# Halved storage of an intermediate, a planner estimate and filler matmuls in a one-core Fourier and mixture kernel

## The chip, the core and the metric

The kernel runs on one core of a Trainium2 chip. The metric is device time in microseconds (us) of one execution; the kernel before has a median of 672.75 us over 3 runs (670.91 to 673.87). Its engines are TensorE (PE, with its weight loads PEld), VectorE (DVE), ScalarE (ACT), GpSimd (POOL) and SyncE (SP), which issues nearly all DMAs.

## The reference

For each of 8 batches, x (3136 x 256) goes through a Fourier transform along its rows, a complex product with a 256 x 256 weight, a soft threshold, and the inverse transform. Then the 128 rows with the best score pass a small feed-forward network.

```python
X = np.fft.rfft(x, axis=1)
Yr = Xr @ w_r - Xi @ w_i + b_r
Yi = Xr @ w_i + Xi @ w_r + b_i
Yr = np.sign(Yr) * np.maximum(np.abs(Yr) - lam, 0.0)   # Yi likewise
y = np.fft.irfft(Y, n=3136, axis=1)
scores = np.einsum('bsd,d->bs', y, w_gate)
for b in range(8):
    top_idx = np.argpartition(-scores[b], 128)[:128]
    h = np.maximum(xe @ w1, 0.0)
    out[b, top_idx] = y[b, top_idx] + g[:, None] * (h @ w2)
```

## The kernel before, in words

The length 3136 is split as 98 x 32 (n1 and n2). Per batch b the work has these stages, and each has a function:

- `x_side` (line 810) loads x in 8 pieces i of 98 partitions x 4 KB (xt tiles, for b = 0 also the cin tiles); `xsum_side` (827) forms sum u and difference v of the two halves (xu, xv; on DVE for b = 0, on POOL after that).
- `s1` (the function that calls `quarters`, 839) does the 98-point transform of piece i in eight fp32 matmul instructions with the constant `first`; ACT copies the result to an at, ot or ct tile and SP stores it to As in DRAM.
- `a_side` (871) reloads As transposed, one av tile per group g of 6, once all 8 pieces are stored. `s2` (886) does the 32-point transform in 64 small fp32 matmuls (px<-fwd,av); ACT and DVE split the result in two fp32r halves (Xh, Xl).
- `spectral` (938) multiplies by w: eight steps k, each of three fp32r matmuls (py<-wh,Xh and so on); at k % 4 == 3 the threshold follows, with the bias tile, on DVE, ACT and POOL.
- `s2i` (985) is the inverse 32-point transform (s<-Y,bwd); ACT copies four banks to a ct tile (128 partitions x 4 x 256), DVE forms the score's part (junk, Csc), and `put` (1009) stores the tile to Cs in DRAM, 512 KB. `s2it` (1015) does the same for a small rest, Ct (64 KB).
- `c_side` (1045) reloads C in four parts i per batch into one of two cin tiles: two transfers of 48 partitions (16 to 63 and 64 to 111), 384 KB each, and a small one from Ct to partitions 15 and 112. `csum_side` (1058) forms sum and difference (cu, cv) of the halves; `s1i` (1073) does the inverse 98-point transform and stores the result.
- `score` (1030), `select`, `fetch` and `ffn` choose the rows, gather them, run the network and scatter the result.

The order of the instructions on every engine is written by a planner while the kernel is built. Every engine wrapper (`Engine.given`, line 223), `mm` (258) and `ld` (292) adds an estimate to a clock for its engine; a side job (`pump`, 377) is taken when its estimated time has come, and the loop at the end picks the stage with the least cost for PE. In `ld` a transfer costs SP 0.4 us, the wire takes bytes / 300e3 us, and the data land 1.2 us after that; a tile's estimated time is the latest of all that wrote it. All engines then run in that order, with semaphores for the data.

`warm` (1312) puts matmuls on constants into a PSUM tile that nobody reads, as many as fit into an estimated wait of PE:

```python
n = int((t - WARM[1] + (0.0 if spec["t"] >= T else WS2 if w else WS) - t0) / (0.23 if w else 0.44))
if t - t0 < WARM[0] or n < 1:
    return
for name, bufs in (("s", SB), ("py", 2)):
    if open_at(name, bufs) <= t0 + 0.3:
```

Here t0 is the estimated end of PE's last matmul and t that at which the next stage can begin. With `WARM[0]` = 99 it always returns at once. It is called (1409) before the first spectral step and, once all 48 groups are through `spectral`, in the rest.

At the start (1341) the rows 0 to 14 of every xt and cin tile are cleared, the first on DVE, the others on POOL, through the wrappers `vec` and `gps`, so that the estimated time of the tile counts them.

Of the kernel before, what the change touches and what calls it, by code (L numbers as in the profile page):

```python
# [10 lines left out]
F32 = mybir.dt.float32  # L11
# [8 lines left out]
B, S, D = 8, 3136, 256  # L20
N1, N2 = 98, 32
H1 = N1 // 2
P0 = 15
PT = P0 + N1
NJ = 24
# [31 lines left out]
def _tables():  # L57
    w = _dft_rows()
    n2 = np.arange(N2)

    f1 = np.zeros((2, H1, 64))
    for i in range(NP):
        for c in range(2):
            f1[0, :, P0 + 2 * i + c] = w[:H1, EVEN[i], c]
            f1[1, :, 1 + 2 * i + c] = w[:H1, ODD[i], c]
    f1[0, :, P0 + 48] = w[:H1, 0, 0]
    f1[1, :, 0] = w[:H1, 49, 0]

    crow = {}
    for j in range(NJ):  # L70
        for kap in range(2):
            g, p, jj = j // 4, j % 4 // 2, j % 2
            k, i = _freq(j, kap)
            crow[k] = _crow(g, kap, p, jj)
            assert j < 12 or crow[N1 // 2 - k] == crow[k]

    i1 = np.zeros((2, H1, 64))
    for par in range(2):
        o = P0 if par == 0 else 0
        for k in EVEN:  # L80
            for c in range(2):
                i1[par, 2 * crow[k] + c, o:o + H1] = w[par::2, k, c]
        i1[par, 48, o:o + H1] = w[par::2, 0, 0]
    first = np.zeros((128, 2, 2, 64))
    for z, t in enumerate((f1, i1)):
        first[P0:64, z] = (np.roll(t, 1, 1) if z else t).transpose(1, 0, 2)
        first[64:PT, z] = t.transpose(1, 0, 2)

    g = np.zeros((NJ, 2, 2, N2, 2, N2))
    gi = np.zeros((6, 2, 2, 2, N2, 2, 2, N2))  # L90
    for j in range(NJ):
        for kap in range(2):
            kk, _ = _freq(j, kap)
            z = -1.0 if kk % 2 else 1.0
            for s in range(N2):
                k = kk + N1 * s
                sg = 1.0 if 2 * k <= S else -1.0
                a = 2 * np.pi * ((n2 * k) % S) / S
                co, si = np.cos(a), np.sin(a)
                g[j, kap, 0, :, 0, s] = co  # L100
                g[j, kap, 1, :, 0, s] = si
                g[j, kap, 0, :, 1, s] = -sg * si
                g[j, kap, 1, :, 1, s] = sg * co
                v = gi[j // 4, j % 4 // 2, kap, j % 2, s]
                v[0, 0] = 2 * co / S
                v[1, 0] = -2 * sg * si / S
                v[0, 1] = z * 2 * si / S
                v[1, 1] = z * 2 * sg * co / S
    g = g.reshape(NJ, 128, 64).transpose(1, 0, 2)

    gi = gi.reshape(6, 2, 128, 2, 2, N2).transpose(2, 0, 1, 3, 4, 5).reshape(128, NJ, 64)

    fr = [(0, N1 * s) for s in range(1, 16)] + [(1, 49 + N1 * s) for s in range(16)] + [(0, 0), (0, S // 2)]
    gt = np.zeros((2, N2, 97))
    git = np.zeros((64, 2, N2))
    for m, (r, k) in enumerate(fr):
        a = 2 * np.pi * ((n2 * k) % S) / S
        co, si = np.cos(a), np.sin(a)
        edge = m > 30
        gt[r, :, 33 + m] = co  # L120
        git[m, r] = (1.0 if edge else 2.0) * co / S
        if not edge:
            gt[r, :, m] = si
            gt[r, :, 66 + m] = -si
            git[33 + m, r] = -2 * si / S

    wq = np.zeros((25, 4, N1))
    order = np.concatenate([np.arange(0, N1, 2), np.arange(1, N1, 2)])
    for j in range(NJ):
        for kap in range(2):  # L130
            k, _ = _freq(j, kap)
            z = -1.0 if k % 2 else 1.0
            col = 4 * (j // 4) + 2 * kap + j % 2
            for c in range(2):
                wq[col, 2 * (j % 4 // 2) + c] = w[order, k, c] * (z if c else 1.0)
    wq[24, 0] = w[order, 0, 0]
    wq[24, 1] = w[order, 49, 0]
    second = np.concatenate([g.reshape(128, -1), gi.reshape(128, -1)], 1)
    tail = np.zeros((64, 97 + 64))
    tail[:, :97] = gt.reshape(64, 97)  # L140
    tail[:, 97:] = git.reshape(64, 64)
    return [a.astype(np.float32) for a in (first.reshape(128, 256), second, tail, wq)]
# [19 lines left out]
def fourier_moe(ctx: ExitStack, tc: tile.TileContext, x, w_r, w_i, b_r, b_i, wg, w1, w2,  # L162
                t_first, t_second, t_tail, t_wq, t_m, t_dig, outs, cap):
    nc = tc.nc
# [5 lines left out]
    dram = ctx.enter_context(tc.tile_pool(name="scratch", bufs=3, space=bass.MemoryType.DRAM))  # L170
# [245 lines left out]
    bias = c_tile([128, 2, D], F32, "bias")  # L416
    bias_t = c_tile([64, D], F32, "bias_t")
    m2l = c_tile([128, 1], F32, "m2l")
    wq = c_tile([25, 4, N1], F32, "wq")
# [564 lines left out]

    def s2i(b, g):
        if g == 0:
            Cs[b] = dram.tile([6, 4, 128, D], F32, name="Cs"), dram.tile([64, D], F32, name="Ct")
            Csc[b] = new(pool, [128, 25], F32, "Csc")
            vec.memset(Csc[b][:, 24:], 0.0)
        for p in range(2):  # L990
            drain(shrinks.pop((b, g, p)))
        y = Y.pop((b, g))
        banks = [new(ps, [128, D], F32, "s", SB) for _ in range(4)]
        for c in range(2):
            for p in range(2):
                for k in range(4):
                    rows = slice(32 * k, 32 * k + 32)
                    mm(banks[k][64 * p:64 * p + 64], bwd[g][rows, 2 * p + c, :], y[rows, p, c, :], c == 0, c == 1, (32 * k, 64 * p))
        t = new(pool, [128, 4, D], F32, "ct", 3)

        def part(k):
            yield "DVE", [banks[k]]
            score_part(b, banks[k], 4 * g + k)

        for k in range(4):
            evict(t[:, k], banks[k])
            hold(banks[k], "s", side(part(k)))

        def put():
            yield "SP", [t]  # L1010
            ld(Cs[b][0][g].rearrange("k p d -> p k d"), t)
            stored["C", b] = stored.get(("C", b), 0) + 1
        hold(t, "ct", side(put()))

    def s2it(b):
        drain(shrinks.pop((b, "t")))
        y = YT.pop(b)
        p = m_tile([64, D])
        mm(p, tail[:, 97:], y)
        t = new(pool, [64, D], F32, "ctt", 1)  # L1020
        act.copy(out=t, in_=p)
        score_part(b, p, 24, 64)

        def put():
            yield "SP", [t]
            ld(Cs[b][1], t)
            stored["C", b] = stored.get(("C", b), 0) + 1
        hold(t, "ctt", side(put()))

    def score(b):  # L1030
        p = m_tile([25, 128])
        turned(p, Csc[b], ident)
        t = new(pool, [25, 4, N2], F32, "sct")
        vec.tensor_copy(t.rearrange("p q n -> p (q n)"), p)
        yield [t]
        p = m_tile([N1, 2, 16])
        for q in range(4):
            mm(p.rearrange("p a n -> p (a n)"), wq[:, q, :], t[:, q, :], q == 0, q == 3)
        vec.tensor_copy(scores[:, b, :].rearrange("p (i a c) -> p a i c", a=2, c=2),
                        p.rearrange("p a (i c) -> p a i c", c=2))  # L1040

# [3 lines left out]
    def c_side():  # L1045
        for b in range(B):
            for i in range(4):
                n = 4 * b + i
                yield "SP", lambda: max(avail(Cs[b]) - EARLY, read.get(key(cts[n % CB]), 0.0)) \
                    if stored.get(("C", b)) == 7 and unused[0] >= 2 * (n - CB + 1) and (0, 7) in summed else None  # L1050
                t = cts[n % CB]
                c = Cs[b][0].rearrange("(q g) k (p a n) d -> a (g k p) q n d", q=2, a=2, n=16)
                for a in range(2):
                    ld(t[16 + 48 * a:64 + 48 * a], c[a, :, :, 4 * i:4 * i + 4, :])
                ld(t[P0::97], Cs[b][1].rearrange("(q a n) d -> a q n d", q=2, a=2)[:, :, 4 * i:4 * i + 4, :])
                stored["c"] = n

    def csum_side():
# [50 lines left out]
    CS, CM = ((0, 8, 9, 10, 11, 12), (11, 12, 13, 14, 14, 14)),42  # L1109
    FB = .25, .5, .75, 1.25, 1.5, 2, 2.5, 3  # L1110
    CN, K0 = 4,4
    WS, WS2 = 1.5, -0.5
    CY = 5, 8, 8, 8, 8, 8, 8, 8
    CX = 10, 10, 10, 10, 11, 11, 11, 12
    WARM = (99, 0.5)
    SP = False
    TB, T1 = -1.5,0.1
    TE, LV, UR, FS, ES, LA, HP = 0,2,0.5,False,True,3,False
# [131 lines left out]
    def middle():  # L1250
# [4 lines left out]
        if k == 8:  # L1255
# [4 lines left out]
                spectral_t(b)  # L1260
                spec["t"], spec["k"] = t + 1, 0
            return t + 1, max(avail(XT[b]), open_at("py")), run, "f"
        if not {"w", "bias"} <= made or (b, g) not in X or (k == 3 and len(Y) > 1):
            return None

        def run():
# [73 lines left out]

    with tc.manual_schedule():
        for z, t in enumerate(xts + cts):
            (gps if z else vec).memset(t[:P0].rearrange("p a c -> p (a c)") if len(t.shape) == 3 else t[:P0].rearrange("p a c d -> p (a c d)"), 0.0)
        ld(first.rearrange("p z c s -> p (z c s)"), t_first)
        side(x_side())
        side(xsum_side())
# [13 lines left out]
        while True:  # L1360
# [40 lines left out]
            if c[1] > now + 0.4:  # L1401
# [3 lines left out]
                if later and min(later) > now + ahead:  # L1405
                    free["PE"] = min(later) - ahead + 0.01
                    continue
            if spec["t"] >= T or at == 0 and (0, 7) in summed:
                warm(c[1])
            if isinstance(c[2], Thread):  # L1410
                if c[2].rank < 0:
# [42 lines left out]
```

## Time and profile before

| | us |
|---|---|
| median of 3 runs | 672.75 (670.91 to 673.87) |
| the profiled execution, its own time | 677.4 |
| its span, first to last instruction | 675.6 |
| PE busy | 633.5 (94% of the span) |
| PEld, DVE, ACT, POOL busy | 407.6, 387.2, 362.6, 394.7 |
| mean granted TensorE clock | 0.978 |

All rows are of one profiled execution. "Busy" is the time in which an engine has an instruction in work; for PE the ends are modelled, so short pauses can hide in it. [...] A bracket behind an instruction says how long its engine stood idle before it and which event ended that; where the engine named had long been done, it was another, often a DMA.

### The profile page before, as it was taken

To read this page: it belongs to the slowest core of one execution; us is meant where nothing else is said; L and a number is where in the kernel's file an instruction comes from. 1 tells how busy PE (TensorE), PEld (TensorE's weight loads), DVE (VectorE), ACT (ScalarE), POOL (GpSimd) and SP (SyncE) were. 2 spreads that over 40 slices of the span, in tenths; PEclk is the share of its full clock that TensorE was granted. 3 is DMA by queue.
4 is the path that set the end of the run, shared out by engine and by line. 5 is a ranking of instruction groups with operands and counts; after the bars stand their busy time and mean duration, and the time that the engine had idled before them with its cause. 6 is when DMAs were issued, how large, how long until landed. Compare 5 with 4: busy or idle time off the path is not lost.

```text
span 675.6 us, 19258 instructions
## 1 busy us (share of the span) xinstructions
PE 633.5 (94%) x7586; PEld 407.6 (60%) x7586; DVE 387.2 (57%) x1208; ACT 362.6 (54%) x779; POOL 394.7 (58%) x337
## 2 busy tenths in 40 slices
PE   6199999999999999999999999999999998799897
PEld 2055755656665656656556666575666665466696
DVE  6123545444457667664667666654667776465742
ACT  4235555557466555656556565566655655444321
POOL 3068443748487656766667466766644656639421
PEclk9679999999999999999999999999999999899999
DMA  8999787989799998897899998897889778478410
GB/s 271 294 247 302 201 273 225 205 282 332 242 268 279 279 313 250 272 296 252 240 276 273 304 266 278 248 306 190 256 241 248 196 223 224 147 177 232 153 39 17
DMA packets 87700, 162.53 MB, mean 241 GB/s; under 512 B 6877, under 2 KB 62010, under 8 KB 87610
## 3 DMA queue, kind: packets, MB, share of 16 engines
q1 hardware_dynamic: 86554, 159.13, 80.1%
q0 software_dynamic: 1056, 2.17, 1.1%
q8 instruction: 60, 0.98, 0.6%
q14 instruction: 30, 0.25, 0.1%
HBM read 83.23 MB, written 78.12 MB: 239 GB/s over the span
## 4 chain that ended last, share of the span: by engine, by line
PE 79%; DMA 7%; issue 5%; DVE 4%; POOL 2%; ACT 1%; SPq 1%; POOLq 0%; DVEq 0%
PE py L272 44%; PE s L272 25%; PE px L272 9%; DMA xe<-in_moe_w 2%; DMA xt<-in_x 2%; DMA av<-As 2%; DMA cin<-Ct 1%; DMA r<-in_w_r 1%; DVE px L220 1%; SPq L301 1%; POOL out L783 1%; DVE c L220 1%; POOL cv L220 1%; DVE py L220 0%; DVE junk L220 0%
## 5 line engine op out<-in xcount | busy, mean ns | idle before, releaser
L220 POOL TENSOR_TENSOR xu<-xt 113x512 f32<-113x512 f32 x56 | 71.9, 1283 | 170.9 <-PE s L272 135.8
L272 PE MATMUL py<-wh,Xh 128*128 128x512 f32 x384 | 169.8, 442 | 1.7 <-ACT Xh L220 1.2
L272 PE MATMUL py<-wl,Xh 128*128 128x512 f32 x384 | 153.0, 398 | 0.0
L272 PE MATMUL py<-wh,Xl 128*128 128x512 f32 x384 | 152.8, 398 | 0.0
L272 PEld LDWEIGHTS py<-wh,Xh 128*128 128x128 f32 x384 | 72.6, 189 | 82.6 <-issue 61.1
L220 DVE TENSOR_TENSOR Xl<-px,Xh 128x512 fp32r<-128x512 f32 x96 | 61.8, 686 | 80.6 <-ACT Xh L220 80.6
L220 POOL TENSOR_TENSOR cu<-cin 113x512 f32<-113x512 f32 x64 | 82.0, 1282 | 41.5 <-PE s L272 39.0
L220 DVE CUSTOM_DVE_ANT_0 junk<-s,wgb 128x256 f32<-128x256 f32 x192 | 80.7, 420 | 32.3 <-ACT ct L220 16.5
L220 ACT COPY ot<-s 113x512 f32<-113x512 f32 x142 | 76.6, 597 | 40.2 <-PE s L272 33.8
L220 ACT COPY at<-s 113x512 f32<-113x512 f32 x110 | 59.2, 592 | 62.4 <-PE s L272 62.4
L272 PEld LDWEIGHTS py<-wl,Xh 128*128 128x128 f32 x384 | 72.8, 189 | 17.3
L220 POOL TENSOR_TENSOR cv<-cin 113x512 f32<-113x512 f32 x64 | 82.1, 1283 | 0.0
L272 PEld LDWEIGHTS py<-wh,Xl 128*128 128x128 f32 x384 | 73.3, 191 | 10.5 <-DVE Xl L220 0.5
L272 PE MATMUL s<-cu,first 64*64 64x512 f32 (+1 forms) x256 | 74.3, 618 | 5.1 <-DVE Csc L220 3.1
L272 PE MATMUL s<-xu,first 64*64 64x512 f32 (+1 forms) x256 | 73.0, 633 | 5.7 <-DVE xu L220 5.7
L272 PEld LDWEIGHTS px<-fwd,av 64*64 64x64 f32 x3072 | 52.1, 137 | 38.0 <-DMA fwd<-t_second 15.7
L220 ACT COPY ct<-s 128x256 f32<-128x256 f32 (+1 forms) x196 | 59.8, 394 | 23.7 <-PE s L272 21.4
L272 PE MATMUL px<-fwd,av 64*64 64x64 f32 x3072 | 56.9, 223 | 16.7 <-DMA av<-As 15.8
L220 POOL TENSOR_TENSOR xv<-xt 113x512 f32<-113x512 f32 x56 | 71.8, 1283 | 0.0
L272 PE MATMUL s<-cv,first 64*64 64x512 f32 (+1 forms) x256 | 71.2, 618 | 0.3 <-POOL cv L220 0.2
L272 PE MATMUL s<-xv,first 64*64 64x512 f32 (+1 forms) x256 | 71.4, 633 | 0.0
L220 ACT ACTIVATE r<-py,m2l 128x512 f32<-128x512 f32 (+1 forms) x58 | 38.3, 660 | 57.2 <-DVE py L220 57.2
(150 smaller groups left out, 968.1 us busy)
## 6 DMA issues: line engine op xcount, KB each, us to landing
out<-ot SPq DMA_DIRECT2D x64, 392.0 KB
av<-As SPq DMA_DIRECT2D x48, 512.0 KB
Cs<-ct SPq DMA_DIRECT2D x48, 512.0 KB
cin<-Cs SPq DMA_DIRECT2D x64, 384.0 KB
xt<-in_x SPq DMA_DIRECT2D x60, 392.0 KB
As<-at SPq DMA_DIRECT2D x55, 392.0 KB
As<-ot SPq DMA_DIRECT2D x7, 392.0 KB
xe<-in_moe_w SPq DMA_DIRECT2D x16, 128.0 KB
```

Of the source, the lines that this page charges most:

```text
L220: return f(*args, **kw)
L272: return nc.tensor.matmul(out, a, b, start=start, stop=stop)
L301: return (eng or nc.sync).dma_start(out=out, in_=src)
L783: nc.gpsimd.indirect_dma_start(out=outs[b], out_offset=bass.IndirectOffsetOnAxis(ap=idx, axis=0), in_=ye, in_offset=None)
```

## The change

C (Cs and Ct) is stored by halves of n2. The columns of the inverse 32-point tables (`gi`, `git`) are put in another order, so that the partitions of a ct tile go (…, n, half); each store becomes two, one of the even and one of the odd partitions (64 partitions x 4 x 1 KB = 256 KB; Ct 32 KB), and a reload fills partitions 16 to 111 of one half of the cin tile with each of its two transfers of 96 partitions, 384 KB as before. The score reads its columns with a step of two. The clearing of rows is issued past the planner's wrappers, so that it counts in no estimate. `warm` is switched on (0.5 in place of 99, with other offsets) and held back as long as pieces of x are summed and not transformed. The spectral steps no longer wait in the plan for the bias, only those with k % 4 == 3 do.

```diff
+    gi = gi.reshape(128, NJ, 2, 2, 16).swapaxes(3, 4).reshape(128, NJ, 64)
+    git = git.reshape(64, 2, 2, 16).swapaxes(2, 3).reshape(64, 2, N2)
...
-            Cs[b] = dram.tile([6, 4, 128, D], F32, name="Cs"), dram.tile([64, D], F32, name="Ct")
+            Cs[b] = dram.tile([2, 2, 3, 4, 64, D], F32, name="Cs"), dram.tile([2, 32, D], F32, name="Ct")
...
-            ld(Cs[b][0][g].rearrange("k p d -> p k d"), t)
+            for a in range(2):
+                ld(Cs[b][0][g // 3, a, g % 3].rearrange("k p d -> p k d"), t[a::2])
...
-            ld(Cs[b][1], t)
+            for a in range(2):
+                ld(Cs[b][1][a], t[a::2])
...
-            mm(p.rearrange("p a n -> p (a n)"), wq[:, q, :], t[:, q, :], q == 0, q == 3)
+            mm(p, wq[:, q, :], t[:, q, :].rearrange("p (n a) -> p a n", a=2), q == 0, q == 3)
...
-                c = Cs[b][0].rearrange("(q g) k (p a n) d -> a (g k p) q n d", q=2, a=2, n=16)
-                for a in range(2):
-                    ld(t[16 + 48 * a:64 + 48 * a], c[a, :, :, 4 * i:4 * i + 4, :])
-                ld(t[P0::97], Cs[b][1].rearrange("(q a n) d -> a q n d", q=2, a=2)[:, :, 4 * i:4 * i + 4, :])
+                c = Cs[b][0].rearrange("q a g k (p n) d -> q (a g k p) n d", n=16)
+                for q in range(2):
+                    ld(t[16:112, q], c[q, :, 4 * i:4 * i + 4, :])
+                ld(t[P0::97], Cs[b][1].rearrange("a (q n) d -> a q n d", q=2)[:, :, 4 * i:4 * i + 4, :])
...
-    WS, WS2 = 1.5, -0.5
+    WS, WS2 = 0.5,0.3
...
-    WARM = (99, 0.5)
+    WARM = (0.5, 0.3)
...
-        if not {"w", "bias"} <= made or (b, g) not in X or (k == 3 and len(Y) > 1):
+        if "w" not in made or (b, g) not in X or k % 4 == 3 and "bias" not in made or (k == 3 and len(Y) > 1):
...
-            (gps if z else vec).memset(t[:P0]...
+            (nc.gpsimd if z else nc.vector).memset(t[:P0]...
...
-            if spec["t"] >= T or at == 0 and (0, 7) in summed:
+            if spec["t"] >= T or at == 0 and (0, 7) in summed and not xuv:
                 warm(c[1])
```

## Rows read from the trace of the kernel before

**Rows 1.** The page: busy shares, then clock and DMA in 40 slices of the span.
```profile
PE 633.5 (94%) x7586; PEld 407.6 (60%) x7586; DVE 387.2 (57%) x1208; ACT 362.6 (54%) x779; POOL 394.7 (58%) x337
...
PEclk9679999999999999999999999999999999899999
DMA  8999787989799998897899998897889778478410
```

**Rows 2.** Stretches: us, then PE, PEld, DVE, ACT, POOL, clock, DMA share, GB/s.
```profile
200.00:300.00 100.00, 99.54 (x1270) 61.01 (x1263) 65.85 (x235) 61.08 (x134) 70.08 (x57) 1.00 0.94 280
...
600.00:615.00 15.00, 13.41 (x105) 11.40 (x102) 9.12 (x29) 5.40 (x9) 7.67 (x7) 1.00 0.89 187
```

**Rows 3.** Timeline of the first wait: start, duration, engine, line, instruction, idle before.
```profile
16.94 1.05 PE L272 MATMUL s<-xv,first 49*64 49x512 f32 x2
...
23.79 0.93 SPq L301 DMA_DIRECT2D av<-As  x2
...
32.84 1.98 PE L272 MATMUL px<-fwd,av 64*64 64x64 f32 x64 [14.83 <-DMA av<-As]
...
35.97 0.79 PE L272 MATMUL py<-wh,Xh 128*128 128x512 f32 x1 [1.15 <-ACT Xh L220]
```

**Rows 4.** Stretches of one us where the granted clock changes.
```profile
21.00:22.00 1.00, 0.00 (x0) 0.00 (x0) 0.00 (x0) 0.00 (x0) 0.00 (x0) 0.94 0.95 371
...
42.00:43.00 1.00, 1.00 (x64) 1.00 (x64) 0.60 (x1) 0.36 (x1) 0.00 (x0) 0.82 0.93 225
```

**Rows 5.** Timeline of the last reloads of C, on SP, POOL and PE.
```profile
594.03 0.40 SPq L301 DMA_DIRECT2D Cs<-ct  x1
...
597.99 1.29 SPq L301 DMA_DIRECT2D cin<-Cs  x2
...
607.16 1.26 POOL L220 TENSOR_TENSOR cu<-cin 113x512 f32<-113x512 f32 x1 [8.11 <-PE s L272]
...
608.47 1.07 PE L272 MATMUL s<-cu,first 64*64 64x512 f32 x2 [1.44 <-POOL cu L220]
609.69 0.64 PE L272 MATMUL s<-cv,first 64*64 64x512 f32 x1
...
627.19 1.28 POOL L220 TENSOR_TENSOR cu<-cin 113x512 f32<-113x512 f32 x1 [2.02 <-DMA cin<-Ct]
...
628.52 1.07 PE L272 MATMUL s<-cu,first 64*64 64x512 f32 x2 [0.58 <-POOL cu L220]
629.74 0.64 PE L272 MATMUL s<-cv,first 64*64 64x512 f32 x1 [0.15 <-POOL cv L220]
```

**Rows 6.** PE's wait at 583 us and the stretch behind it.
```profile
585.00:600.00 15.00, 13.59 (x103) 6.62 (x103) 6.61 (x26) 8.66 (x20) 8.73 (x8) 0.77 0.58 179
...
586.25 1.08 PE L272 MATMUL s<-cu,first 64*64 64x512 f32 x1 [3.06 <-DVE Csc L220]
```

**Rows 7.** Stretches in which x, As and C are loaded, for their DMA rate.
```profile
5.70:11.00 5.30, 5.30 (x25) 1.97 (x26) 4.01 (x7) 2.09 (x4) 1.25 (x1) 1.00 0.91 292
...
28.00:29.00 1.00, 0.00 (x0) 0.00 (x0) 0.00 (x0) 0.00 (x0) 0.00 (x0) 0.50 1.03 349
...
602.00:605.00 3.00, 3.00 (x28) 3.00 (x27) 2.40 (x8) 1.21 (x3) 0.00 (x0) 1.00 0.98 154
```

**Rows 8.** The chain that ended last: start, duration, engine, tile, instructions.
```profile
36.80 5.06 PE py L272 x11
...
58.44 1.09 PE px L272 x64
...
446.42 1.88 PE s L272 x16
...
451.99 4.40 PE py L272 x18
```

**Rows 9.** SP's issues of C's stores: count, ns at least, median and most.
```profile
L301 SPq DMA_DIRECT2D Cs<-ct x48: 359/382/1332, 67.2 to 594.0; - x48
```

**Rows 10.** The page's groups: weight loads of the py steps, busy us and mean ns.
```profile
L272 PEld LDWEIGHTS py<-wh,Xh 128*128 128x128 f32 x384 | 72.6, 189 | 82.6 <-issue 61.1
```

More of the change, by code (lines that the diff above doesn't have):

```diff
@@ L1342, in fourier_moe @@
         for z, t in enumerate(xts + cts):
-            (gps if z else vec).memset(t[:P0].rearrange("p a c -> p (a c)") if len(t.shape) == 3 else t[:P0].rearrange("p a c d -> p (a c d)"), 0.0)
+            (nc.gpsimd if z else nc.vector).memset(t[:P0].rearrange("p a c -> p (a c)") if len(t.shape) == 3 else t[:P0].rearrange("p a c d -> p (a c d)"), 0.0)
         ld(first.rearrange("p z c s -> p (z c s)"), t_first)
```

## The prediction, made before the changed kernel was run

> **What bounds the kernel now.** I read the page first, then stretches, then the chain and the timelines. PE is busy for 94% of the span, and the DMA engines for eight to nine tenths of most slices [rows 1]. Between 200 and 300 us PE works 99.54 of 100 us, at full clock [rows 2]: there every other engine and every transfer has slack, and only fewer PE instructions or a higher clock could save time. So I look for places where PE waits or runs at half clock. There are three.
>
> The first is the start. PE ends the last transform of the first batch at 16.94 + 1.05 = 18.0 us and stands until 32.84, 14.8 us, because the reload of As, issued at 23.79, lands only then [rows 3]. The granted clock falls at about 21.9 us, 3.9 us into that wait, and is full again only at about 42.4 (0.82 in that us; half before) [rows 4]. In between s2 and the first spectral steps run at half clock.
>
> The second is the tail's use of C. The reload of the last batch is issued at 597.99; POOL forms its first sum only at 607.16 (the PE work its bracket names had long ended, so it waited for the DMA), and PE waits for both halves of it. At 628.52 the same happens again, where POOL names the small load behind the reload of C [rows 5].
>
> The third is a 3.06 us wait for the score's DVE parts at 586.25, which drags the mean clock of 585 to 600 down to 0.77 [rows 6].
>
> **Why C is slow.** From 602 to 605 us, when C is loaded into 48 partitions at a time, the DMA engines are 0.98 busy and move 154 GB/s; As into 128 partitions went at 349 (1.03 busy) and x into 98 at 292 [rows 7]. Busy engines with half the bytes say that the destination holds them up. [...]
>
> **The change, part by part.**
>
> *Reload in transfers of 96 partitions.* Bytes and runs (4 KB) stay. A part of C is 2 x 384 + 16 = 784 KB: 5.1 us at 154 GB/s. The new rate is not in the trace; its nearest row is x (98 partitions, also 4 KB runs) at 292, its lower bound 187 (600 to 615 us, C mixed with output stores [rows 2]), its upper 349. I take 280, a little under x: 2.8 us, 2.3 less. Over 32 reloads that frees 74 us of transfer, but in the steady stage PE hides all of it [rows 2]: 0 there, at most -2 us (PE's 0.46 us idle per 100, over 450). In the tail it lies on the path: in front of the first s1i PE loses 1.44 us before cu and 609.69 - 608.47 - 0.47 = 0.75 before cv (0.47 being four of the sixteen in a group of 1.88 [rows 8]); at the second 0.58 + 0.75 = 1.33. Together 3.5 us. With the reload landing 3 us earlier at the first (a saved 2.3 and what C's next part no longer takes from it), cu and cv end at about 606.8, where PE arrives at 607.0; at the second the POOL sums have 2.02 us of DMA wait to give back. I take -3.5, between 0 and -3.5. Next late would be the POOL sums themselves, 1.27 us each.
>
> *Stores in two.* 48 + 8 more issues on SP, some 0.38 us each [rows 9], 21 us over the span; the bytes are the same. SP is in order, so what stands behind them (reloads of As, loads of x, output stores) goes out 0.38 us later; the second av tile, the four xt tiles and the second cin tile, loaded a step ahead, hide that (were each of the 48 on the path, it would be 18 us). Only the last store and its rest, at 594.03, lie on the path to the reload: 0.4 + 0.5 us later. That moves cv's end at the first wait to 607.7, where PE comes to cv at 607.03 + 0.47 = 607.5: 0.2 at most, taken as 0, and 0.9 if the reload is not faster.
>
> *The score's columns with a step of two; tables in another order.* Four matmuls of 32 columns per batch, the same count: 0.
>
> *Filler in the first wait.* How many matmuls go in follows from the planner's own formulas. With the cleared rows out of the estimate, x's last piece lands at 1.3 + 0.44 (the constant `first`) + 8 x 1.338 (401 KB at 300 KB per us) + 1.2 = 13.6; DVE's eight pairs of sums, 1.38 us each from 4.3, end at 15.4, and PE at 16.4. The eight stores of As then keep the wire until 23.6, the constants (0.92 MB) until 26.7, av until 28.4; plus 1.2 is 29.6. The planned wait is 13.2 us (with the clearing counted it is 10.1, because x's last pieces go to the cin tiles, which POOL clears last). The count is (13.2 + 0.2) / 0.44 = 30 fp32 matmuls of 256 columns. No row has this form. Nearest is the group of s1i [rows 8]: 16 instructions of 512 columns in 1.88 us, four side by side, so 0.47 per 512 columns; a filler matmul is two instructions of 256, 0.47 at most and, without the group's change-over, about 0.43. So 30 last 12.9 to 14.1 us, end at 31.0 to 32.2, before the data at 32.84, and leave a pause of 0.7 to 1.9 us, shorter than the 3.9 after which the clock fell. The wait itself does not shrink; the order of the loads before av stays.
>
> Gain: the 64 matmuls of s2 take 1.09 instead of 1.98 us, and eleven spectral ones 11 x 4.40/18 = 2.7 instead of 5.06 [rows 8]: -3.3. Against this stands a second filler between s2 and the first spectral step: in the plan of the kernel before that wait is 2.98 us, so some 12 fp32r matmuls of 0.244, 2.9 us, where X is really complete 1.98 us after s2 (35.97 - 34.82 = 1.15 for the first half, 36.80 for all [rows 3, 8]). They are in PE's queue ahead of the spectral steps: +1.0. I take -2.3, between 0 (if batch 1's transfers, 0.9 busy there, are late instead) and -3.3.
>
> *Filler in the tail.* `warm` needs all four s banks or both py banks free. At 583 us PE waits for just those s banks, and py still holds the last thresholds, so nothing goes in and the half clock stays: 0. A mean of 0.77 over 15 us is 6.9 us at half clock [rows 6]; were it filled, at most half of these, -3.4, would be saved. A few fillers of one matmul elsewhere cost 0.24 us each at most, +1.
>
> *Bias.* It had landed before X, so the freed steps start no earlier: 0. Its DMA keeps its place.
>
> **The sum.** -2.3 - 3.5 = -5.8 on an execution of 677.4 us (span 675.6), which is 4.65 above the median of 672.75. I carry the difference over: 667.0.
>
> **The rivals.**
>
> *The first wait's clock falls after all.* The fill ends more than 3.9 us before the data, if fewer than about 25 go in. Then s2 and spectral run at half clock as before, and the second fill, 12 at 0.46 us, costs 5.5 - 2.0 = 3.5: -3.5 + 3.5, 672.7. For it: planned times and real ones differ by some us. Against: the formulas leave 30. Chance 0.14.
>
> *The tail does not follow.* The selection of rows, a chain of DVE and PE steps up to the last gathers, ends the tail rather than C; then only the start's -2.3 stays: 670.5. For it: DVE is the other engine PE waits for [rows 6]. Against: PE loses time at C's own steps, and the selection's matmuls stand in the same queue behind them [rows 5]. Chance 0.13.
>
> *Slower: the first fill outlasts the wait.* PE is in order, so s2 starts only when the last filler is done. The point is 14.8 / 30 = 0.49 us per filler matmul. If weight loads do not hide (0.19 us each in the py steps [rows 10], two per filler), a filler takes 0.43 + 0.38 = 0.81 and thirty 24.3, 9.5 us too long; less a start gain of 2.3 and a tail gain of 3.5 this is 672.75 + 9.5 - 5.8 = 676.5. For it: no row has a 128 x 128 fp32 stream. Against: the py stream hides its loads at 0.244 per matmul [rows 8]. Chance 0.09.
>
> **How the numbers follow.** The forecast, both gains, has the remaining 0.64. A measurement of this kernel can tell about 0.5%, 3.4 us: faster is below 669.4. The forecast's cases and a little of the second rival give faster 0.66; the first two rivals are within, 0.25; the third is slower, 0.09. The range: low is -3.3 - 3.5 - 3.4 and half of the steady stage's 2, -11.2, 661.5; high takes in the first two rivals and some scatter from a plan whose order shifts, 673.5. That leaves out the slower one and the tails.
>
> **What would show it.** Right: some 60 PE instructions py<-first of 256 columns from 18 us, ended before 32.84; the clock 1.00 from 20 to 50 us; eleven spectral matmuls in under 3 us; stretches of C loads over 240 GB/s at the same DMA share; no wait over 0.3 us before s<-cu in the last 70 us; still about 0.77 at 585 to 600. Wrong: PE's s2 later than 33 us, the clock at 0.5 anywhere before 50, C's rate still below 200, or new waits of PE between 100 and 540 us.

## The result, and the profile of the changed kernel

The changed kernel takes 664.75 us (median of 4 runs, 663.25 to 665.95) where the kernel before, run beside it, takes 672.09 (670.91 to 673.87). The ratio is 0.9896, 95% interval 0.9867 to 0.9926: by the ratio 7.0 us faster, between 5.0 and 8.9. Predicted were 667.0 and -5.8. The profiled execution takes 664.63 us; its span is 662.9 against 675.6, 12.7 us less. The two profiles therefore differ by 5 to 6 us more than the medians; where that comes from is told below.

First the page of the changed kernel: busy times, the granted clock in tenths of TensorE's full speed, DMA share, and the queue of the ordinary transfers with its packets, MB and share of the 16 engines' span.

```profile
PE 641.9 (97%) x7650; PEld 415.9 (63%) x7650; DVE 388.1 (59%) x1208; ACT 362.6 (55%) x779; POOL 394.7 (60%) x337
...
PEclk9999999999999999999999999999999999999999
DMA  8999977989699978897789888896767776487410
...
q1 hardware_dynamic: 87450, 159.13, 76.4%
```

The same queue of the kernel before:

```profile
q1 hardware_dynamic: 86554, 159.13, 80.1%
```

The clock's gaps [rows 1] are gone in this execution. The same bytes hold the DMA engines for 76.4% of a shorter span, where it was 80.1%: 506 us in place of 541, 35 less. PE has 64 instructions more: 56 of the first wait's filler and 8 in the tail.

The timeline of PE in the first wait of the changed kernel:

```profile
17.94 12.35 PE L275 MATMUL py<-first 128*128 128x256 f32 x56
30.23 1.16 PE L275 MATMUL px<-fwd,av 64*64 64x64 f32 x64
32.55 0.50 PE L275 MATMUL py<-wh,Xh 128*128 128x512 f32 x1 [1.16 <-ACT Xh L223]
33.38 0.50 PE L275 MATMUL py<-wh,Xl 128*128 128x512 f32 x1 [0.34 <-DVE Xl L223]
...
36.15 1.16 PE L275 MATMUL px<-fwd,av 64*64 64x64 f32 x64
```

28 fillers of 0.44 us run from 17.94 to 30.3. s2 follows at once, at a clock of 1.00, in 1.16 us where it took 1.98 [rows 3]. Eleven spectral matmuls lie between 33.38 and 36.22, 2.84 us, where they took 5.06 [rows 8]. Between s2 and the first spectral step nothing was put in. The 64 instructions of s2's next group begin at 36.15, before at 41.79: 5.64 us won, of which 2.61 are an earlier start of s2 (32.84 to 30.23), since As landed earlier in this execution, at 29.69 us where it was 32.70.

Stretches of the changed kernel, columns as in [rows 2]: the steady stage, the stretch behind the selection's wait, and the reload of C.

```profile
200.00:300.00 100.00, 99.54 (x1224) 59.91 (x1224) 67.44 (x239) 58.99 (x129) 67.36 (x54) 1.00 0.89 279
...
585.00:600.00 15.00, 15.00 (x114) 10.44 (x113) 10.50 (x31) 6.95 (x13) 7.58 (x7) 1.00 0.70 214
...
591.00:595.00 4.00, 4.00 (x37) 4.00 (x35) 3.34 (x9) 1.65 (x4) 0.09 (x1) 1.00 0.95 261
```

The first 7.5 us of that reload, in the kernel before and in the changed one:

```profile
598.50:606.00 7.50, 7.50 (x61) 6.41 (x61) 5.51 (x18) 3.34 (x6) 0.55 (x1) 1.00 1.01 190
```

```profile
588.50:596.00 7.50, 7.50 (x58) 6.09 (x58) 5.68 (x18) 3.18 (x6) 1.69 (x2) 1.00 0.94 258
```

In the steady stage PE is busy for the same 99.54 of 100 us as before [rows 2], with a DMA share of 0.89 where it was 0.94. In the middle of a reload C comes at 261 GB/s where it was 154 [rows 7]; from the reload's start on it is 258 against 190. The half clock of 0.77 behind 585 us [rows 6] is gone as well, which was not forecast.

Up to 621 us PE's instructions stand in the same order in both kernels but for the 28 fillers, so each can be set beside its twin: the s2 group of 89.14 begins at 83.38 (5.76 earlier), the px<-cnt of 570.88 at 563.50 (7.38), the s1i of 586.25 at 577.30 (8.95), the s<-Y of 591.39 at 580.53 (10.86). From 90 to 540 us the lead of any kernel below over the profile of before, row by row of PE, changes by 0.5 us at most. All is won or lost ahead of 90 us and behind 540.

### The profile page after: what moved, and what is told of

Its sections match the earlier page's. It is cut to its first block, busy times and chain, and to the rows that moved or that the text cites. A ratio compares the mean times of both kernels' runs of the same rounds, so it can differ in the third digit from the quotient of the medians.

```text
span 662.9 us, 19427 instructions
## 1 busy us (share of the span) xinstructions
PE 641.9 (97%) x7650; PEld 415.9 (63%) x7650; DVE 388.1 (59%) x1208; ACT 362.6 (55%) x779; POOL 394.7 (60%) x337
## 3 DMA queue, kind: packets, MB, share of 16 engines
q1 hardware_dynamic: 87450, 159.13, 76.4%
## 4 chain that ended last, share of the span: by engine, by line
PE 82%; DVE 5%; issue 5%; DMA 4%; POOL 2%; ACT 1%; SPq 1%; POOLq 0%; DVEq 0%
PE py L275 45%; PE s L275 27%; PE px L275 10%; DMA av<-As 2%; DMA xe<-in_moe_w 1%; DVE px L223 1%; DVE c L223 1%; SPq L304 1%; DMA xe<-out,idxs 1%; POOL xe L694 1%; POOL out L786 1%; DVE n L223 1%; DMA xt<-in_x 1%; DVE r L223 0%; DVE py L223 0%
## 5 line engine op out<-in xcount | busy, mean ns | idle before, releaser
L223 DVE CUSTOM_DVE_ANT_0 junk<-s,wgb 128x256 f32<-128x256 f32 x192 | 80.8, 421 | 29.9 <-ACT ct L223 16.1
L275 PE MATMUL s<-cu,first 64*64 64x512 f32 (+1 forms) x256 | 72.5, 603 | 1.0 <-DVE Csc L223 1.0
L275 PE MATMUL s<-cv,first 64*64 64x512 f32 (+1 forms) x256 | 69.7, 604 | 0.0
L223 POOL TENSOR_TENSOR Y<-r,r 128x512 f32<-128x512 f32 x46 | 59.2, 1287 | 10.3 <-DMA out<-ot 4.6
```

Of the source, the lines that this page charges most:

```text
L223: return f(*args, **kw)
L275: return nc.tensor.matmul(out, a, b, start=start, stop=stop)
```

## The experiments

The kernels ran in three groups; those of a group, and the kernel before beside them, shared a chip, another in each group. Ratios are to the kernel before in the same group. Its medians were 672.45, 676.92 and 672.11. The first row of the table is the run of the result, with the kernel before that was run beside it. "Fill" counts the filler matmuls of the first wait. Behind a row stand 12 runs, but 4 of the changed kernel, 6 each of r_after, e5_48 and e7_short, 7 of e10_old4 and 9 of b1_const.

| kernel | fill | reload of C | ratio (95%) | queue q1 |
|---|---|---|---|---|
| changed | 28 | new, 96 partitions | 0.9896 (0.9867 to 0.9926) | 76.4% |
| r_after, the same | 28 | new, 96 | 0.9875 (0.9830 to 0.9919) | 76.3% |
| e6_notail | 28 | new, 96 | 0.9915 (0.9888 to 0.9941) | 76.7% |
| e5_48 | 28 | new, 4 x 48 by turns | 0.9895 (0.9857 to 0.9934) | 78.3% |
| e10_old4 | 28 | old layout, 4 x 48 by turns | 0.9919 (0.9888 to 0.9950) | 77.7% |
| b1_const | 26 | new, 96 | 0.9907 (0.9877 to 0.9938) | 76.1% |
| e7_short | 18 | new, 96 | 0.9900 (0.9862 to 0.9939) | 76.5% |
| e8_est | 23 | new, 96 | 0.9940 (0.9916 to 0.9963) | 76.1% |
| e3_nofill | 0 | new, 96 | 0.9934 (0.9911 to 0.9958) | 77.0% |
| e1_layout | 0 | new, 96 | 0.9944 (0.9918 to 0.9970) | 77.1% |
| e4_long | 38 | new, 96 | 1.0004 (0.9970 to 1.0037) | 76.5% |
| e2_start | 28 | old, 2 x 48 | 0.9979 (0.9951 to 1.0007) | 80.6% |
| e9_rows | 28 | new layout, 2 x 48 | 1.0024 (1.0001 to 1.0047) | 81.0% |

My theory (A) was that the start gains through the clock, the tail through the reload, and that the two add up. The rivals: the start's gain is only an earlier landing of As; the tail's is the planner's new order or the tail's filler.

### First group: each half alone, no filler, a longer filler

e1_layout: the kernel before with the hunks of the layout alone (the two lines on tables, Cs and Ct, stores, reload, score):

```diff
-            Cs[b] = dram.tile([6, 4, 128, D], F32, name="Cs"), dram.tile([64, D], F32, name="Ct")
+            Cs[b] = dram.tile([2, 2, 3, 4, 64, D], F32, name="Cs"), dram.tile([2, 32, D], F32, name="Ct")
...
-            ld(Cs[b][0][g].rearrange("k p d -> p k d"), t)
+            for a in range(2):
+                ld(Cs[b][0][g // 3, a, g % 3].rearrange("k p d -> p k d"), t[a::2])
```

> The kernel before with C's layout, stores in two, reload by 96 partitions and the score's column order alone; no filler, old estimates. Theory A (start and tail gain separately: the clock at the start, the faster reload in the tail): the tail's part alone, 672.1 - 4 = 668, C's reload at over 240 GB/s, PE's waits before s<-cu in the tail under 2 us, the start as before (clock at one half from about 22 to 42 us). Rival B (the tail's gain came from the planner's new order and the filler there, not from the reload): 671 to 673. Rival C (the layout is the whole gain, the start's is noise of the profiled run): 665.

e2_start: the changed kernel with all hunks of the layout taken back, such as:

```diff
-                for q in range(2):
-                    ld(t[16:112, q], c[q, :, 4 * i:4 * i + 4, :])
+                for a in range(2):
+                    ld(t[16 + 48 * a:64 + 48 * a], c[a, :, :, 4 * i:4 * i + 4, :])
```

> The changed kernel with C's old layout (old tables, one store, reload by 48 partitions): the filler at the start and in the tail, the estimate and the bias condition stay. Theory A: the start's gain alone, 672.1 - 3.3 = 668.8, clock 1.00 from 20 to 50 us; C's reload at about 154 GB/s again and over 4 us of PE's waits before s<-cu in the tail. Rival B (planner and filler make the tail's gain): 665. Rival C: 672.

e3_nofill:

```diff
-            if spec["t"] >= T or at == 0 and (0, 7) in summed and not xuv:
+            if spec["t"] >= T:
```

> The changed kernel without the 28 filler matmuls at the start; all else stays, the order of PE's other work too. Theory A (the clock): the clock falls in the first wait, s2 takes 1.98 us and the first spectral half 5.06 as before: 664.8 + 3.3 = 668.1. Rival C (the start's gain is As landing earlier, by chance or by order): 664.8, with s2 beginning at about 30.2 us as in the changed kernel. If s2 begins at 32.8 again, the late landing belongs to the program without filler.

e4_long:

```diff
-    WS, WS2 = 0.5,0.3
+    WS, WS2 = 4.9,0.3
```

> The changed kernel with 38 filler matmuls in place of 28: ten more of 0.44 us, the fill ends 4.4 us later, at 34.6. Theory A with the data landing at 30.2 in every run: s2 starts 4.4 us later and all of it reaches the end: 669.2. If As lands at 32.8 in most executions: only 1.8 more, 666.6. If a delay at the start is made up later (PE waits there for the next loads anyway): 664.8.

**The layout alone** gave 669.07 us, 0.9944: 3.8 us. Its PE has exactly the order of the kernel before, so neither the planner nor filler made this. **The start alone** gave 671.61, 0.9979, an interval that holds no change; theory A had 668.8, and this is the number of rival C (672), whose numbers for e1_layout (665) and e3_nofill (664.8) did not come. **Without the start's filler** the changed kernel took 669.19, 0.9934. **The longer fill** took 672.37, 1.0004, 3.2 us more than theory A had.

PE's timeline at s2 in e3_nofill:

```profile
31.24 1.99 PE L275 MATMUL px<-fwd,av 64*64 64x64 f32 x64 [12.45 <-DMA av<-As]
```

and in e4_long:

```profile
18.63 16.67 PE L275 MATMUL py<-first 128*128 128x256 f32 x76
35.23 1.16 PE L275 MATMUL px<-fwd,av 64*64 64x64 f32 x64
```

Without filler, s2 runs at half clock (0.50 from 31 to 34 us) and its data come at 31.24, not at 32.84 as in the profile of before. In all the other profiles here, the last part of As for s2 lands between 29.7 and 32.0 us; in e1_layout, whose start is that of the kernel before, at 30.3. So 32.84 was a late landing of that one execution, and part of the 5.64 us above belongs to it, as the rival said. But the filler is worth something too: 0.9934 and 0.9896 differ by 2.6 us, though on two chips and with intervals that overlap. The profiles say it more plainly. From the last transform of batch 0 to 540 us, PE gains 3.6 to 6.6 us on the profile of before in the seven with a fill of 28 and 1.8 to 4.0 in the four with none or one of 18 or 23; the means, 4.8 and 2.8, are 2.0 us apart. With the longer fill all ten matmuls lie on the path. s2 begins 5.0 us later than in the changed kernel (0.7 of it because the fill itself began later), and PE is still 4.6 us behind it at 540 us: a delay at the start goes through. At the end it is 7.0 behind. Of the 2.4 more, 0.9 went near a wait for gathered rows at 588 us and 1.5 at a wait of 1.58 us before a py<-av,w1h at 651.9, which the changed kernel does not have; why they are there is not shown.

Now the tail. ACT's copy of the feed-forward network's second weights to w2h, and PE's wait for the counts of the selection, in the kernel before:

```profile
567.47 0.41 ACT L220 CAST w2h<-xe 128x256 fp32r<-128x256 f32 x1 [0.82 <-DMA xe<-in_moe_w]
...
570.88 0.21 PE L272 MATMUL px<-cnt,tm 98*98 98x4 bf16 x2 [1.38 <-DVE cnt L220]
```

the same with the start's filler and the old layout (e2_start), and its wait for C:

```profile
564.68 0.41 ACT L220 CAST w2h<-xe 128x256 fp32r<-128x256 f32 x1 [1.68 <-DMA xe<-in_moe_w]
...
568.09 0.25 PE L272 MATMUL px<-cnt,tm 98*98 98x4 bf16 x2 [2.25 <-DVE cnt L220]
...
602.56 1.07 PE L272 MATMUL s<-cu,first 64*64 64x512 f32 x2 [0.74 <-POOL cu L220]
```

and in the changed kernel:

```profile
560.08 0.42 ACT L223 CAST w2h<-xe 128x256 fp32r<-128x256 f32 x1
...
563.50 0.21 PE L275 MATMUL px<-cnt,tm 98*98 98x4 bf16 x2 [0.45 <-DVE cnt L223]
```

Here is a part of the tail's gain that I had not seen. The weights are loaded behind a reload of C (issued at 561.23 and 559.21 in the kernel before). ACT's copy there waits 0.82 us for them; the relu (r<-py) that stands behind the copy in ACT's order begins at 567.78, 0.31 us after it, then come DVE's Y and Csc, then cnt at 570.67, and PE, which has waited 1.38 us. In the changed kernel the copy does not wait, and PE waits 0.45. In the three profiles with the slow reload PE loses 1.38 to 2.28 us there; in nine of the eleven with a fast one it loses 0.45 or 0.46, in e3_nofill 0.73 and in e5_48 1.01. The wait for cu of the first of these transforms, 0.74 us here, is gone in the changed kernel, and no other fast reload has more than 0.25. For e2_start I had expected over 4 us of waits before s<-cu: they were 1.4 with those before s<-cv. The chain that ended last in the kernel before had shown it, 6.21 us of xe<-in_moe_w:

```profile
561.23 6.21 DMA xe<-in_moe_w
```

It shows too one reason why the two halves don't simply add up. In e2_start PE is 3.5 us ahead of the profile of before at 560 us and only 1.3 ahead of it at 575: its wait at px<-cnt is 2.25 us where the profile of before has 1.38, and the first eight fp32r matmuls behind that wait start 0.45 us apart on the mean, 0.24 in the profile of before.

### Second group: what makes the reload fast, a shorter fill, fewer bytes ahead of As

r_after is the changed kernel itself.

> The changed kernel itself once more, beside the next three on the same chip, as their yardstick. Theory A: 664.8 within 1.5 us, the clock 1.00 through the first wait. If it is at 667 or more, its first four runs were on the low side and the differences to the kernels without filler (669.2) and with a longer one (672.4) shrink.

e5_48:

```diff
-                    ld(t[16:112, q], c[q, :, 4 * i:4 * i + 4, :])
+                    for z in range(0, 96, 48):
+                        ld(t[16 + z:64 + z, q], c[q, z:z + 48, 4 * i:4 * i + 4, :])
```

> The changed kernel with each reload of 96 partitions split in two of 48 (four per part of C, two issues more on SP, some 0.4 us each); DRAM layout, stores in two, filler and the order of PE's work stay. Theory P (the number of partitions that one transfer writes sets the rate): about 154 GB/s at a full DMA share again, the waits of the tail come back, 664.8 + 3.8 = 668.6. Rival S (the order in DRAM or the stores in two set it): the rate stays over 240 GB/s and the time at 664.8 to 665.5.

e7_short:

```diff
-    WS, WS2 = 0.5,0.3
+    WS, WS2 = -3.9,0.3
```

> The changed kernel with 18 filler matmuls in place of 28: the fill ends at about 26 us, 4.3 to 5.2 before As has landed in the profiles so far (30.2 to 31.2). Theory A: the clock falls before s2 as it did 3.9 us into the wait of the kernel before, s2 takes 1.98 us, and the time is that without filler, 669.2. Rival: any filler does, since the pause is only a third of the old one: 664.8.

b1_const:

```diff
-    CS, CM = ((0, 8, 9, 10, 11, 12), (11, 12, 13, 14, 14, 14)),42
+    CS, CM = ((0, 9, 9, 10, 11, 12), (11, 12, 13, 14, 14, 14)),42
-    CA = 1, 8, 8, 12, 11, 0, 12
+    CA = 1, 8, 9, 12, 11, 0, 12
```

> The changed kernel with the bias and the second fwd tile (384 KB) loaded behind the first reload of As instead of ahead of it; the filler falls to 26 by the planner. Theory A (the start is bound by what the DMA engines move ahead of As, and a delay there reaches the end, as the longer fill showed): As lands 384/300 = 1.3 us earlier, s2 begins at about 29.2 and the time is 664.8 - 0.9 = 663.9. Rival (the transfers of batch 1 or the bias are then late and take it back): 664.8 or more, with a new wait of PE between 35 and 60 us.

On this chip all is some 4 us slower, the kernel before too (676.92). The profile of r_after (median 669.15) shows where. PE's wait before s1i:

```profile
579.36 0.61 PE L275 MATMUL s<-cu,first 64*64 64x512 f32 x1 [3.41 <-issue]
```

and the stretch around it:

```profile
580.00:595.00 15.00, 15.00 (x99) 7.62 (x97) 6.16 (x22) 8.07 (x18) 7.44 (x6) 0.66 0.48 149
```

In the first profile of the changed kernel the same matmul waited less, and the clock stayed:

```profile
577.30 0.61 PE L275 MATMUL s<-cu,first 64*64 64x512 f32 x1 [1.04 <-DVE Csc L223]
```

This is the wait of [rows 6], with the fall of the clock behind it, in the changed kernel. The four profiles of this group have it at 2.49 to 3.41 us, those of the other two groups and the first one of the changed kernel at 1.04, with old and new layout alike. The profile of before, with 3.06 and its own 677.4 us, is of this kind. So the 0.77 of before and its absence after are no work of the change: the two profiles differ there by some 4 us that the medians don't have. In the one case ACT starts its copies of the s banks some 2 us late (the view says only "remote"). By the semaphore events in the traces it waits there for PE: the signal of the s<-Y matmuls comes 2.1 us behind their modelled end in the profile of before (585.25 against 583.19) and 2.4 behind it in r_after, but within 0.1 in the first profile of the changed kernel. What makes PE late stays open.

**e5_48** kept the speed, 670.07 us, 0.9895. The stretch of its reload:

```profile
596.00:600.00 4.00, 4.00 (x37) 4.00 (x35) 3.32 (x10) 1.64 (x4) 0.45 (x1) 1.00 1.00 246
```

246 GB/s in transfers of 48 partitions. That the width of one transfer sets the rate (theory P) is refuted. **e7_short** took 670.73, 1.6 us more than r_after, inside both intervals; s2 came 4.66 us after the fill and took 1.98 us, as at the clock of 0.50 in e3_nofill:

```profile
18.26 8.04 PE L275 MATMUL py<-first 128*128 128x256 f32 x36
30.96 1.98 PE L275 MATMUL px<-fwd,av 64*64 64x64 f32 x64 [4.66 <-DMA fwd<-t_second]
```

**b1_const** gained nothing (670.99). The bias then reached DVE only at 43.28 us:

```profile
43.28 0.64 DVE L223 TENSOR_SCALAR bias<-bias 128x512 f32<-128x512 f32 x1 [9.26 <-DMA bias<-in_b_i]
```

but PE had other work by then and shows no wait over 0.2 us between 35 and 60, so the rival that was named does not hold as it stands. As did come earlier: its last part for s2 landed at 29.9, in r_after at 30.5, although x came 0.9 us later in this execution. What held s2 was the fill of 26, which ran to 31.0:

```profile
29.75 1.24 PE L275 MATMUL py<-first 128*128 128x256 f32 x5
30.92 1.16 PE L275 MATMUL px<-fwd,av 64*64 64x64 f32 x64
```

So whether an earlier As, with a fill to match, is worth anything was not tested.

### Third group: the source or the destination, the tail's filler, the estimate

e9_rows:

```diff
-                c = Cs[b][0].rearrange("q a g k (p n) d -> q (a g k p) n d", n=16)
-                for q in range(2):
-                    ld(t[16:112, q], c[q, :, 4 * i:4 * i + 4, :])
+                c = Cs[b][0].rearrange("q a g k (p n) d -> (a g k p) q n d", n=16)
+                for a in range(2):
+                    ld(t[16 + 48 * a:64 + 48 * a], c[48 * a:48 * a + 48, :, 4 * i:4 * i + 4, :])
```

> The changed kernel with the reload taken from the new order in DRAM but written as the kernel before wrote it: two transfers of 48 partitions, each with both halves of four groups (2 x 4 KB per partition), first all of partitions 16 to 63, then all of 64 to 111. Theory H (the rate falls when all engines write one half of the partitions for long; four short transfers by turns, as in the last experiment, are enough to avoid it): 157 to 190 GB/s at a full DMA share, ratio to the kernel before 0.993 to 0.998, as the changed kernel with the old layout. Theory D (the distance between the 4 KB pieces in DRAM, 32 KB in the old order and 16 KB in the new, sets it): 246 to 261 GB/s and a ratio of 0.987 to 0.990, as the changed kernel.

e10_old4, against e2_start:

```diff
-                for a in range(2):
-                    ld(t[16 + 48 * a:64 + 48 * a], c[a, :, :, 4 * i:4 * i + 4, :])
+                for q in range(2):
+                    for a in range(2):
+                        ld(t[16 + 48 * a:64 + 48 * a, q], c[a, :, q, 4 * i:4 * i + 4, :])
```

> The changed kernel with C's old order in DRAM and one store, its reload in four transfers of 48 partitions that take the lower and the upper partitions by turns. Theory H: 240 GB/s or more, ratio 0.987 to 0.991: the new layout was not needed, a finer split of the old reload does it. Theory D: 157 to 190 GB/s, ratio 0.993 to 0.998.

e6_notail:

```diff
-            if spec["t"] >= T or at == 0 and (0, 7) in summed and not xuv:
+            if at == 0 and (0, 7) in summed and not xuv:
```

> The changed kernel without filler in the tail (8 matmuls of 512 columns between 621 and 645 us, and the PSUM banks that follow from them); the start's filler and the layout stay, and PE's order up to 621 us is the same. Theory A (they cost and give nothing): the ratio of the changed kernel, 0.987 to 0.990. Rival: their 8 x 0.24 us lie on the path, 1 to 2 us faster without them; or the clock falls in the tail's last waits without them, 1 to 3 us slower.

e8_est:

```diff
-            (nc.gpsimd if z else nc.vector).memset(t[:P0].rearrange("p a c -> p (a c)") if len(t.shape) == 3 else t[:P0].rearrange("p a c d -> p (a c d)"), 0.0)
+            (gps if z else vec).memset(t[:P0].rearrange("p a c -> p (a c)") if len(t.shape) == 3 else t[:P0].rearrange("p a c d -> p (a c d)"), 0.0)
```

> The changed kernel with the cleared rows back in the planner's estimate of x's landing: 23 filler matmuls in place of 28, all other work in the same order. The fill ends 2.2 us earlier, at 28.1 to 28.9, some 2 to 3 us before As. Theory A (a pause shorter than 3.9 us leaves the clock as it is): s2 takes 1.16 us at the same start, the ratio is 0.987 to 0.990. Rival (this pause adds to the waits behind s2 and the clock falls in the first spectral steps): 1 to 2.5 us slower than the changed kernel, 0.990 to 0.993. Rival (the fill of 28 outlasts the data by some tenths, so a shorter one is better): up to 0.7 us faster.

The stretch in which C is reloaded in e9_rows:

```profile
595.50:599.50 4.00, 4.00 (x37) 4.00 (x35) 3.33 (x10) 1.67 (x3) 0.00 (x0) 1.00 1.02 173
```

and in e10_old4:

```profile
594.00:598.00 4.00, 4.00 (x36) 4.00 (x36) 3.34 (x9) 1.65 (x4) 0.00 (x0) 1.00 1.02 223
```

This settles the order in DRAM against the way the transfers are divided. The new order in DRAM, written to SBUF as the kernel before wrote it, is slow: 173 GB/s, 672.82 us, 1.0024, with PE's waits back, as its timeline shows:

```profile
569.47 0.21 PE L275 MATMUL px<-cnt,tm 98*98 98x4 bf16 x2 [2.28 <-DVE cnt L223]
...
602.92 1.07 PE L275 MATMUL s<-cu,first 64*64 64x512 f32 x2 [1.24 <-POOL cu L223]
```

The old order in DRAM, written by turns to the lower and the upper partitions, is fast: 223 GB/s, 666.40 us, 0.9919. Both come out as theory H had it in kind and a little beside its numbers (a ratio of at most 0.998, and a rate of at least 240). Neither the layout nor the 96 partitions were needed for the gain; dividing the old reload in four does it, within the interval.

What exactly is slow in the old form stays open between two readings: all DMA engines write one half of the partitions for 384 KB at a stretch, or each transfer brings two 4 KB pieces to the same partition. e5_48 and e10_old4 change both at once, and with them the order in which a transfer reads its pieces from DRAM; no run here separates them. The reload of As also brings several pieces to each partition, of 1 KB, at 349 GB/s over 128 partitions [rows 7], which speaks for the first reading and does not show it.

**e6_notail**: 665.65, 0.9915; the tail's filler is worth nothing that can be told. **e8_est**: 667.91, 0.9940, as without any filler, and against its theory A, which held a pause under 3.9 us for harmless. The fill of 23 ended 3 us too early:

```profile
18.39 10.20 PE L275 MATMUL py<-first 128*128 128x256 f32 x46
31.59 1.99 PE L275 MATMUL px<-fwd,av 64*64 64x64 f32 x64 [3.00 <-DMA fwd<-t_second]
```

s2 takes 1.99 us, and the first spectral steps are at half clock (0.50 from 33 to 37 us and from 38 to 40). By the traces it is the changed estimate of x's landing, 28 matmuls in place of 23, that lets the filler hold the clock; in time the two are 1.7 us apart, with intervals that overlap.

No kernel here beats the changed one by more than the intervals.

## Why the prediction was right, and where it was not

**What bounds the kernel.** Right: the start, the reload of C in the tail, and nothing between. The steady stage's 0 held: PE's share between 200 and 300 us did not move. The 74 us less transfer of my sum were 35 by the queue's share, 1.1 us per part of C in place of 2.3: I had taken the 154 GB/s of the middle of a reload for the whole of it, which moves 190 in its first 7.5 us.

**Reload.** -3.5 was forecast, e1_layout measured -3.8 (-2.0 to -5.5). The rate was taken as 280 and is 261 (245 in e1_layout). The place was right in the main: row by row, the changed kernel's profile gains 2.2 us on that of before at the first of the two transforms (2.19 forecast) and 0.8 at the second (1.33 forecast), and waits for cu or cv nowhere behind 590 us. What I passed over are 1.3 us at px<-cnt, which hang on the same transfers through ACT's copy of the weights. Between 560 us and the end, seven profiles with a fast reload and the 1.04 us wait gain 4.1 to 7.1 us on the profile of before, mean 5.8; the two with a slow one gain 2.5 and 3.0. The difference of 3.0 agrees with the term.

The reason was wrong. I had ascribed the 154 GB/s to the destination alone, because 98 and 128 partitions were filled at 292 and 349 [rows 7], and taken any transfer of 48 partitions to be slow; the 246 of e5_48 show that short transfers to the two halves by turns are not. Two long ones from the same order in DRAM came at 173 (e9_rows); why they are slower is not shown.

**Filler in the first wait.** Forecast: 30 matmuls of 0.43 to 0.47 us, ending at 31.0 to 32.2. It was 28 of 0.44, ending at 30.3. The saved time on s2 and the spectral steps, 0.82 + 2.22 us, is the forecast 3.3 less 0.3. Three things came otherwise:

- The second filler, +1.0 for twelve matmuls before the first spectral step, did not go in. I took the planned wait from the kernel before and left out that `not xuv` bars filler as soon as sums of batch 1 stand ready.
- In its place, some executions pay another way. With the fill of 28 the clock stays at 1.00 between 33 and 45 us in the profiles of the changed kernel, r_after and e10_old4, and falls to 0.50 for some 3 us in those of e2_start, e5_48, e6_notail and e9_rows (in e2_start from 36 to 39), behind the pauses of 1.15 and 0.34 us that follow s2. What tells the executions apart is open. From 34 to 37 us in e6_notail, columns as in [rows 2], the clock third from the end:

```profile
34.00:37.00 3.00, 3.00 (x9) 2.33 (x8) 0.00 (x0) 0.00 (x0) 2.90 (x3) 0.50 1.04 260
```

- I held a pause shorter than 3.9 us for harmless, because the clock fell 3.9 us into the wait of before. After 3.00 us in e8_est it was at half. The margin here was smaller than my sum had it.

The net -2.3 came out near all the same, in part by luck, since a cost that did not come was replaced by one that I had not thought of: 2.6 us between e3_nofill and the changed kernel, 1.7 between e8_est and e6_notail and 1.6 between e7_short and r_after of one group each, each pair with intervals that overlap, and 2.0 between the means of the profiles.

**The sum.** -5.8 against -7.0, by adding the terms. They don't add so plainly, and that the sum came near is luck to that extent: with the slow reload the filler is worth 1.4 us (e2_start, interval over zero) or less (e9_rows), with the fast one 1.7 to 2.6. The profile of e2_start shows some of it taken back (3.5 us ahead at 560, 1.3 at 575), 0.9 by the longer wait at px<-cnt and 1.5 behind that wait, but how much of the difference between 3.8 and the 7 us that lie between e9_rows and e10_old4 this explains is not settled.

**Stores in two.** 0 is neither refuted nor shown. With the slow reload, e9_rows (stores in two) is 3.0 us behind e2_start (one store), by ratios on two chips with intervals that overlap; the forecast had 0.9 for that case. With the fast one, e5_48 (two) is not behind e10_old4 (one). The price per issue was mis-sized: SP takes 0.61 us for each of the 96, not 0.38 [rows 9], though each moves half the bytes: 58 us of SP in place of 18, beside other work all the same.

```profile
L304 SPq DMA_DIRECT2D Cs<-ct x96: 585/608/1386, 63.0 to 583.7; - x96
```

**Tail filler and clock behind 585 us.** Nothing went in at the selection's wait, as forecast, and 8 matmuls elsewhere cost nothing that can be told. The half clock that should have stayed was gone in the first profile and back in r_after: I read a wait whose length changes from one group, and chip, to the next as one of the program.

**Bias.** Right: it was ready at 28.8 us.

**The rivals.** The clock that falls after all is e8_est, five matmuls away, at 1.7 us and not the 3.5 of a second fill. The fill that outlasts the wait is e4_long, ten away. Between them the fill of 28 ends from 0.5 us before the landing of As to 1.2 us after it in its seven profiles. That the tail doesn't follow is refuted by e1_layout.

## What to carry to other kernels

When DMA engines are busy and move half the bytes that they move elsewhere, divide the transfer otherwise before the data are laid out anew: four transfers by turns (223 GB/s in e10_old4, 179 in e2_start with the two of before, the DMA engines 1.02 busy both times) did here what a new layout in DRAM was made for. A filler had to end close to the end of its wait here: from 0.5 us before it to 1.2 after it held the clock at 1.00 through s2, five matmuls fewer (3.0 us before, e8_est) lost the gain, and ten more (e4_long) took as much as the whole change gives. So the estimate of the wait is the thing to get right. Follow a late transfer through the order of every engine behind it; the wait that it costs may stand at a selection that never touches the data, as PE's 1.38 us at px<-cnt in the kernel before.

## What the runs showed of the hardware

- With the same order in DRAM, C came at 173 GB/s in two transfers of 48 partitions with two 4 KB pieces each (e9_rows), at 246 in four of one piece by turns (e5_48), at 261 in two of 96 (the changed kernel), the DMA engines 0.95 to 1.02 busy each time.
- PE's wait before s1i in the tail was 1.04 us in the first profile of the changed kernel and in the eight of the first and third groups, 2.49 to 3.41 in the four of the second group, on another chip, and 3.06 in the profile of before; with one and the same program it was 1.04 and 3.41. The median of the kernel before was 4.5 to 4.8 us higher beside the second group than beside the others.
- After a fill that ended 3.00 us before s2 (e8_est), s2 took 1.99 us and the clock was 0.50 from 33 to 37 us; after pauses of 0.35 and 0.54 us (e10_old4, e2_start), s2 took 1.16 at 1.00. In four of the seven profiles with a fill of 28 the clock then fell to 0.50 all the same for some 3 us, behind pauses of 1.15 and 0.34 us.
- SP took 0.38 us (median) for each of 48 stores of 512 KB, and 0.61 us for each of 96 stores of 256 KB from every second partition.
